# A dynamic convolution with a gated projection on one core: taps over pairs of groups, products grouped by tiling

## The chip, the core and the metric

The kernel runs on one core of a Trainium2 chip. The time is what one execution takes on the device, in microseconds (us). Three executions of the kernel before took 504.61, 506.79 and 507.75 us; their median, 506.79 us, is the time before.

## What is computed

The input x has 8 lanes (the batch) of 4224 positions of 192 channels, in fp32. Cut to what matters, the reference is:

```python
w = softmax(weight_gen, axis=-1)                   # 8 lanes x 4224 x 8 heads x 7 taps
x_unf[b, s, k] = x_pad[b, s + k]                   # 7 taps back in time, 24 channels per head
y = einsum('bshk,bskhg->bshg', w, x_unf)           # the dynamic convolution
for k in range(5): gate_pre += conv_w[k] * y_pad[:, k:k + S, :]
gate = 1 / (1 + exp(-gate_pre))
out = (gate * (y @ w_val)) @ w_out                 # w_val, w_out: 192 x 192
```

## The kernel before, in words

The sequence is cut into 36 groups of positions, g0 to g35: the first has 88, the last 56, all others 120. A group goes through these steps, for all 8 lanes at once.

**The softmax side.** weight_gen comes in 18 parts (p0 to p17). For each, VectorE takes the maximum, subtracts it, sums the exponentials, takes the reciprocal and normalises (lines 247 to 270), and ScalarE takes the exponential (257). SyncE's queue copies six rows between neighbours (the halo of a part, 241 and 242), ScalarE spreads the weights into lines with zeros between them (287), SyncE stores these lines to DRAM (304) and loads them back in slanted order into one of two tiles tb (351): so each group gets band matrices.

**The banks (365).** TensorE multiplies x of the group with its band matrices, in four banks of 32 matmul instructions each, in tiles of 32 columns. kind 0 and 1 hold heads 0 to 3 of lanes 0 to 3 and 4 to 7, kind 2 heads 4 and 5, kind 3 heads 6 and 7. They are made in the order 3, 2, 0, 1. ScalarE copies each bank out of PSUM (384): 0 and 1 into ringA, 2 into ringB, 3 into a tile S. Twelve small DMAs on POOL's queue then move pieces of S into rows of ringA and ringB that the 24-channel heads leave free (393, 395). Each bank takes one of three PSUM tiles of the pool ps_a in turn, so that the fourth bank of a group takes the tile of the first.

**The gate.** Tap 0 of the 5 taps is a ScalarE copy with a scale (413), taps 1 to 4 are VectorE multiply-adds (420) on an accumulator, aA (960 columns) for ringA and aB (480) for ringB. Then ScalarE takes the Sigmoid (425). The rings hold three groups in a row; where a group stands at the front, a copy of four columns makes the halo (400).

**The values and the outputs.** The value product (441 to 448) multiplies ringA and ringB with w_val: wva uses the whole array, wvd too, wvm tiles of 64 columns, wvb tiles of 64 rows. VectorE multiplies gate and value (459, 461). The output product (omm) is made in two halves k; each has a B part (485, tiles of 64 rows) and an A part (478, whole array). ScalarE copies it out (499, 496 for half of the last group) and SyncE stores it (511, 509).

**The order.** Nothing is scheduled by a tool: every step is put into a list with a planned time, and the list is sorted. Planned group m starts at when(m), 12.9 us after the one before; stage(m, t, ...) puts a step at when(m) + t. The engines follow the resulting order each in its own queue and wait for each other. Softmax steps of VectorE take the places (2.3, 10.4, 13.6) of each planned period, exponentials 7.05, spreads 5.0 or 11.6. The value product of a group stands one period after its banks, its outputs two periods after:

```python
stage(m + 1, 9.2, g.sigm, 1)
stage(m + 1, 10.4, g.sigm, 0)
stage(m + 1, 6.05 if m < NM - 1 else 3.6, g.val)
for k, t in ((0, 3.7), (1, 10.7))[:g.halves]:
    stage(m + 2, t, g.omm, k)
```

Of the kernel before, what the change touches and what calls it, by code (L numbers as in the profile page):

```python
# [17 lines left out]
def tile_dynconv_gated_moe(  # L18
# [15 lines left out]
    nc = tc.nc  # L34
# [36 lines left out]
    LP = HALO + 3 * NB  # L71
# [5 lines left out]
    ps_a = ctx.enter_context(tc.tile_pool(name="ps_a", bufs=3, space=bass.MemoryType.PSUM))  # L77
    ps_v = ctx.enter_context(tc.tile_pool(name="ps_v", bufs=1, space=bass.MemoryType.PSUM))
    ps_o = ctx.enter_context(tc.tile_pool(name="ps_o", bufs=1, space=bass.MemoryType.PSUM))
# [5 lines left out]
    ringA = const.tile([P, L, LP], FP32, name="ringA")  # L85
    ringB = const.tile([P, LH, LP], FP32, name="ringB")
# [9 lines left out]
    un01 = work.tile([P, 2, 2 * D], FP32, name="ot", bufs=4).bitcast(U32)  # L96
    un = [un01[:, :, 0:D], un01[:, :, D:2 * D], const.tile([P, 2, KC], U32, name="un")]
    raw_t = const.tile([P, 4 * NWT], FP32, name="raw")
# [208 lines left out]
    class Group:  # L307

        def __init__(self, m):
# [5 lines left out]
            self.p0 = HALO + NB * (m % 3) + (NB - self.n if m == 0 else 0)  # L315
            self.pa = {}
# [36 lines left out]
        def bank(self, kind):  # L353
# [6 lines left out]
            pa = ps_a.tile([P, 512], FP32, name="pa")  # L360
# [25 lines left out]
        def move(self, k, u):
            eng = nc.sync if self.m >= NM - 2 and u else nc.gpsimd
            g, q, ch = HOLE[k]
# [3 lines left out]
            if g == 0:  # L392
                eng.dma_start(out=ringA[q:q + h, LH * u:LH * u + LH, p0:p0 + n], in_=self.S[p:p + h])  # L393
            else:
                eng.dma_start(out=ringB[HD * u + q:HD * u + q + h, :, p0:p0 + n], in_=self.S[p:p + h])  # L395

        def halo(self, g):
            if self.m and self.m % 3 == 0:
                r = (ringA, ringB)[g]
                nc.scalar.copy(out=r[:, :, 0:HALO], in_=r[:, :, LP - HALO:LP])  # L400

        def src(self, g, j):
            p = self.p0 - HALO + j
            return (ringA, ringB)[g][:, :, p:p + self.n]

        def tap0(self, g):
            self.halo(g)
            n = self.n
            if g == 0:
                self.aA = work.tile([P, L * NB], FP32, name="aA", bufs=3)[:, 0:L * n]  # L410
            else:
                self.aB = work.tile([P, LH * NB], FP32, name="aB", bufs=3)[:, 0:LH * n]
            nc.scalar.activation(out=self.lanes(self.acc(g)), in_=self.src(g, 0), func=AF.Copy, scale=cw[:, g, 0:1])  # L413

        def acc(self, g):
            return self.aA if g == 0 else self.aB

        def tap(self, g, j):
            a = self.lanes(self.acc(g))
            nc.vector.scalar_tensor_tensor(out=a, in0=self.src(g, j), scalar=cw[:, g, j:j + 1], in1=a,  # L420
                                           op0=ALU.mult, op1=ALU.add)

        def sigm(self, g):
            a = self.acc(g)
            nc.scalar.activation(out=a, in_=a, func=AF.Sigmoid)  # L425

        def val(self):
            n = self.n
            if self.m == NM - 1:
                v2, *v01 = [ps_a.tile([P, 512], FP32, name="pa") for _ in range(3)]  # L430
            else:
                v2 = ps_v.tile([P, 512], FP32, name="v2")
                v = ps_v.tile([P, 2, 512], FP32, name="v01")
                v01 = [v[:, u] for u in range(2)]
                self.both = v
            self.v2, self.v01 = v2, v01
            A, Bt = self.src(0, HALO), self.src(1, HALO)
            A = [A[:, LH * u:LH * u + LH] for u in range(2)]
# [276 lines left out]
```

## Time and profile before

| | |
|---|---|
| median of three executions | 506.79 us |
| the profiled execution | 508.85 us |
| its span in the profile | 507.1 us |
| TensorE, VectorE, ScalarE, POOL busy | 467.9, 415.7, 337.1, 282.6 us |
| mean granted clock of TensorE | 0.972 of full speed |
| moved by DMA | 108.76 MB |

The profile is of one execution. PE is TensorE's matmuls, PEld its weight loads, DVE VectorE, ACT ScalarE, SPq the issues of SyncE's queue; L365 is line 365. A row of a timeline has the start in us from the span's start, the duration in us, the engine, the line, the operation, the tiles it writes and reads, the shape, the number of instructions merged into it, and in brackets the idle time before it with what released it. Matmuls are pipelined, so the distance between two starts says more than a duration. The rows named in the prediction stand in a section of their own below.

### The profile page before, as it was taken

Reading aid. Unit: us, or ns where it says so; the run is one execution under the profiler, and the core shown is the slowest. Engines: PE = TensorE matmul, PEld = TensorE weight load, DVE = VectorE, ACT = ScalarE, POOL = GpSimd, SP = SyncE. Lnnn points to the kernel's source line nnn. Section 1 sums busy time; section 2 is a strip of 40 time slices with the busy share of each in tenths; the row PEclk is TensorE's granted clock in tenths of the full one; section 3 lists DMA queues with packets and bytes.
Section 4 is the critical chain, followed back from the end, with each engine's and each line's share of the span. In section 5 each row is a group of like instructions: output and inputs, shape, how many; then the busy total and the mean of one; then the engine's idle time right before and its main releaser. Section 6 shows DMA issues by size and latency. Waiting matters only on the chain.

```text
span 507.1 us, 16002 instructions
## 1 busy us (share of the span) xinstructions
PE 467.9 (92%) x6338; PEld 330.2 (65%) x6338; DVE 415.7 (82%) x494; ACT 337.1 (66%) x524; POOL 282.6 (56%) x488
## 2 busy tenths in 40 slices
PE   9427699999999999999999999989999999999994
PEld 5325567666676767767677767757677776677663
DVE  7867789889896898898989899879879786677871
ACT  7346488968689468594959495759595565655632
POOL 9457545556564656556465656546566655556210
PEclk9867899999999999999999999999999999999989
DMA  6999999899899979798899999987978888886322
GB/s 202 224 198 276 235 211 239 228 217 224 205 221 257 230 190 212 233 267 210 232 251 252 235 250 226 233 218 199 223 219 225 208 206 222 232 223 183 94 76 90
DMA packets 117222, 108.76 MB, mean 214 GB/s; under 512 B 51920, under 2 KB 108363, under 8 KB 117149
## 3 DMA queue, kind: packets, MB, share of 16 engines
q1 hardware_dynamic: 96685, 74.37, 58.2%
q0 software_dynamic: 20464, 33.38, 26.7%
q8 instruction: 50, 0.82, 0.7%
q14 instruction: 23, 0.19, 0.1%
HBM read 60.39 MB, written 38.94 MB: 196 GB/s over the span
## 4 chain that ended last, share of the span: by engine, by line
DMA 39%; issue 14%; ACT 12%; POOL 12%; PE 11%; DVE 9%; SPq 2%; ACTq 0%; DVEq 0%; POOLq 0%
DMA ringB<-S 11%; DMA xt<-in_x_dram 10%; POOL ringA L393 9%; DMA ringA<-S 9%; DVE aA L420 5%; PE po L478 3%; DMA tb<-z 3%; PE pa L365 3%; DMA out_dram<-ot 3%; ACT zt L287 3%; DVE aB L420 2%; DMA wt<-in_weight_gen_dram 2%; PE po L485 2%; ACT L257 2%; DMA wt<-wt 1%
## 5 line engine op out<-in xcount | busy, mean ns | idle before, releaser
L393 POOL DMA_DIRECT2D ringA<-S x280 | 151.2, 546 | 99.5 <-DMA ringB<-S 30.2
L420 DVE SCALAR_TENSOR_TENSOR aA<-ringA,wf,aA 128x960 f32<-128x960 f32 (+2 forms) x144 | 171.3, 1190 | 38.4 <-ACT aA L413 31.9
L365 PE MATMUL pa<-tb,xt 126*32 126x120 f32 (+2 forms) x4608 | 137.5, 274 | 30.5 <-DMA tb<-z 19.4
L365 PEld LDWEIGHTS pa<-tb,xt 126*32 126x32 f32 (+2 forms) x4608 | 124.1, 111 | 43.0 <-issue 28.4
L395 POOL DMA_DIRECT2D ringB<-S x140 | 77.4, 557 | 91.7 <-ACT ringB L384 50.5
L420 DVE SCALAR_TENSOR_TENSOR aB<-ringB,wf,aB 128x480 f32<-128x480 f32 (+2 forms) x144 | 100.4, 697 | 16.5 <-ACT aB L413 14.3
L478 PE MATMUL po<-wf,aA 128*120 128x192 f32 (+2 forms) x560 | 112.0, 344 | 0.0
L478 PEld LDWEIGHTS po<-wf,aA 128*120 128x120 f32 (+2 forms) x560 | 90.6, 191 | 16.4 <-issue 13.6
L499 ACT COPY ot<-po 120x768 f32<-120x768 f32 (+1 forms) x69 | 55.4, 803 | 22.9 <-PE po L478 22.6
L425 ACT ACTIVATE aB<-aB 128x480 f32<-128x480 f32 (+2 forms) x36 | 21.5, 598 | 66.0 <-DVE aB L420 65.9
L441 PE MATMUL v<-ringA,wva 128*128 128x480 f32 (+1 forms) x140 | 62.4, 568 | 1.0 <-DMA ringB<-S 0.8
L485 PE MATMUL po<-wf,aB 64*120 64x192 f32 (+2 forms) x560 | 61.4, 338 | 0.0
L413 ACT ACTIVATE aA<-ringA,wf 128x960 f32<-128x960 f32 (+2 forms) x36 | 38.9, 1081 | 33.2 <-DMA ringA<-S 27.0
L485 PEld LDWEIGHTS po<-wf,aB 64*120 64x120 f32 (+2 forms) x560 | 46.8, 185 | 21.2 <-issue 18.2
L459 DVE TENSOR_TENSOR aA<-v,aA 128x960 f32<-128x960 f32 (+1 forms) x35 | 40.1, 1145 | 6.5 <-ACT aA L425 6.1
L425 ACT ACTIVATE aA<-aA 128x960 f32<-128x960 f32 (+2 forms) x36 | 35.8, 994 | 11.1 <-DVE aA L420 11.0
L287 ACT COPY zt<-wt 128x256 f32<-128x256 f32 (+3 forms) x80 | 37.5, 550 | 8.5 <-DVE wt L270 6.4
L448 PE MATMUL v<-ringB,wvb 64*128 64x480 f32 (+1 forms) x140 | 37.4, 611 | 0.0
L384 ACT COPY ringA<-pa 128x480 f32<-128x480 f32 (+2 forms) x72 | 35.9, 546 | 2.0 <-PE pa L365 2.0
L441 PEld LDWEIGHTS v<-ringA,wva 128*128 128x128 f32 x140 | 26.0, 193 | 16.4 <-issue 15.5
L327 POOL DMA_DIRECT2D xt<-in_x_dram x34 | 31.0, 911 | 9.5 <-DVE aA L459 3.8
L444 PE MATMUL v<-ringA,wvm 128*64 128x480 f32 (+1 forms) x140 | 35.7, 588 | 0.0
(84 smaller groups left out, 391.4 us busy)
## 6 DMA issues: line engine op xcount, KB each, us to landing
xt<-in_x_dram POOLq DMA_DIRECT2D x32, 768.0 KB, 7.9
out_dram<-ot SPq DMA_DIRECT2D x136, 180.0 KB
tb<-z SPq DMA_DIRECT2D x228, 88.0 KB
z<-zt SPq DMA_DIRECT2D x14, 576.0 KB
wt<-in_weight_gen_dram SPq DMA_DIRECT2D x14, 448.0 KB
ringA<-S POOLq DMA_DIRECT2D x268, 15.0 KB, 4.7
z<-zt SPq DMA_DIRECT2D x3, 800.0 KB
wt<-wt SPq DMA_DIRECT2D x14, 157.5 KB
```

Source lines behind the costliest of these rows:

```text
L287: nc.scalar.copy(out=dst, in_=src)
L365: nc.tensor.matmul(out=pa[Q * c:Q * c + Q, n * l:n * l + n], lhsT=self.xb[0:k, x0:x0 + Q], rhs=self.t[0:k, LH * u + l, PAD // 2:(PAD + n) ...
L393: eng.dma_start(out=ringA[q:q + h, LH * u:LH * u + LH, p0:p0 + n], in_=self.S[p:p + h])
L395: eng.dma_start(out=ringB[HD * u + q:HD * u + q + h, :, p0:p0 + n], in_=self.S[p:p + h])
L413: nc.scalar.activation(out=self.lanes(self.acc(g)), in_=self.src(g, 0), func=AF.Copy, scale=cw[:, g, 0:1])
L420: nc.vector.scalar_tensor_tensor(out=a, in0=self.src(g, j), scalar=cw[:, g, j:j + 1], in1=a, op0=ALU.mult, op1=ALU.add)
L425: nc.scalar.activation(out=a, in_=a, func=AF.Sigmoid)
L441: nc.tensor.matmul(out=v01[u][:, 0:w], lhsT=wva, rhs=A[u], start=True, stop=False)
L459: nc.vector.tensor_tensor(out=a, in0=self.both[:, :, 0:w], in1=a, op=ALU.mult)
L478: nc.tensor.matmul(out=po[0:n, u, D * t:D * t + D], lhsT=gA[:, u, k, t], rhs=woa, start=first and t == 0, stop=not first, skip_group_check ...
L485: nc.tensor.matmul(out=po[0:n, u, D * t:D * t + D], lhsT=gB[hs, k, t], rhs=wob[hs], start=first and t == 0, stop=not first, skip_group_che ...
L499: nc.scalar.copy(out=self.ot[0:n], in_=self.po[0:n, :, 0:2 * D])
```

## The change

- Taps: ringA and ringB get four slots, one for each group modulo 4, each with its own halo. An even group and the next odd one stand side by side; tap 0, the taps and the Sigmoid of the two are one instruction each, with twice the columns (1920 and 960). The first and the last two groups stay single. Halo copies are made for every pair.
- Values are made three periods behind the banks (two for the first two groups), outputs one period after them. At the end of the list the values of the last four groups and the outputs of the last five follow in turn.
- PSUM: one pool with tiles c (banks 3 and 0), v2 (bank 1 and the B values), v01 (the A values), x0 and x1 (the two halves of the output; x1 also bank 2).
- The products are split by tiling: both B parts of the output and wvb, then both A parts, wva, and last wvd with wvm.
- Softmax places move to (4.9, 10.4, 13.6), with places of their own in the first three periods; exponentials of later parts stand in even periods only. The tile ot has three buffers (before: four). The moves of the last group and the last stores are spread over three queues.

The core of the diff:

```diff
-    LP = HALO + 3 * NB
+    LP = HALO + NB
...
-    ringA = const.tile([P, L, LP], FP32, name="ringA")
-    ringB = const.tile([P, LH, LP], FP32, name="ringB")
+    ringA = const.tile([P, 4, L, LP], FP32, name="ringA")
+    ringB = const.tile([P, 4, LH, LP], FP32, name="ringB")
...
+            self.fast = m // 2 in (0, NM // 2 - 1)
...
-            pa = ps_a.tile([P, 512], FP32, name="pa")
+            pa = pair("x1")[:, 0] if kind == 2 else psum.tile([P, 512], FP32, name="v2" if kind == 1 else "c")
...
+            if self.m == NM - 1 and k < 4:
+                eng = (nc.gpsimd, nc.sync, nc.scalar)[(k + u) % 3]
...
-            if self.m and self.m % 3 == 0:
-                r = (ringA, ringB)[g]
-                nc.scalar.copy(out=r[:, :, 0:HALO], in_=r[:, :, LP - HALO:LP])
+            r, e = (ringA, ringB)[g], self.m % 4
+            if self.m % 2 == 0:
+                for a, b, n in ((1, 2, 2),) if e else ((3, 0, 1),) * (self.m > 0) + ((0, 1, 1),):
+                    nc.scalar.copy(out=r[:, b:b + n, :, 0:HALO].rearrange("p e l c -> p (e l) c"),
+                                   in_=r[:, a:a + n, :, NB:LP].rearrange("p e l c -> p (e l) c"))
...
+        def span(self, g, j):
+            if self.fast:
+                return self.src(g, j), self.lanes(self.acc(g))
+            i, e = (ringA, ringB)[g], self.m % 4
+            return (i[:, e:e + 2].rearrange("p e l c -> p (e l) c")[:, :, j:j + NB],
+                    self.sums[g].rearrange("p e (l n) -> p (e l) n", n=NB))
...
+        def val_w(self):
+            self.both = v = pair("v01")
             for u in range(2):
                 hs = slice(HD * u, HD * u + HD)
+                nc.tensor.matmul(out=v[:, u, 0:LH * self.n], lhsT=wvb[hs], rhs=self.src(1, HALO)[hs],
+                                 start=True, stop=False, tile_position=(HD * u, 0))
...
-            b_part(True)
-            a_part(False)
...
-                        nc.sync.dma_start(out=dst, in_=self.ot[h * e:h * e + h, u])
+                        (nc.gpsimd if e == 2 else (nc.scalar, nc.sync)[u]).dma_start(out=dst, in_=self.ot[k][h * e:h * e + h, u])
...
-    JOB, DENSE, EXP, SPREAD = (2.3, 10.4, 13.6), 0, (7.05,), (5.0, 11.6)
+    JOB, EXP, SPREAD = (4.9, 10.4, 13.6), (7.05,), (5.0, 11.6)
...
+    FIRST = ((10.4, 13.6), (4.9, 7.6, 10.4, 13.6), (2.3, 4.9, 6.0, 8.0, 10.4, 13.6))
...
-            at(slot(t, EXP), s.exp)
+            at(slot(t, EXP, 1 if i < 8 else 2), s.exp)
...
+        q = m // 2 * 2 + 2
+        if m < 2:
+            q = m + 1
+            stage(q, 1.5, g.tap0, 1)
+            stage(q, 2.15, g.tap0, 0)
...
+        elif m % 2 == 0:
+            end = m == NM - 4
+            stage(q, 1.5, g.tap0, 1)
+            stage(q, 2.65 if end else 4.85, g.tap0, 0)
+            for j in range(1, KC):
+                stage(q, (1.6, 3.0, 12.5, 13.6)[j - 1] if end else (1.6, 3.2, 3.3, 14.0)[j - 1], g.tap, 1, j)
+                stage(q, (2.7, 3.1, 12.4, 13.5)[j - 1] if end else (6.5, 12.5, 15.6, 17.4)[j - 1], g.tap, 0, j)
+            for k, t in ((1, 5.0), (0, 9.7)):
+                stage(q + 1, 5.6 - 0.1 * k if end else t, g.sigm, k)
+        late = m + 3 - (NM - 1)
+        if late >= 0:
+            t = 3.0 + 9.0 * late
+            stage(NM - 1, t, g.val_w)
+            stage(NM - 1, t + 0.1, g.val_a)
+            stage(NM - 1, t + 0.2, g.val_m)
...
+        else:
+            v = m + (3 if m > 1 else 2)
+            stage(v, 5.2, g.val_w)
+            stage(v, 8.6, g.val_a)
+            stage(v, 10.2, g.val_m)
+            stage(v, 11.7, g.gv, 0)
+            stage(v, 12.4, g.gv, 1)
...
+                stage(v + 1, 3.7 + 0.75 * k, g.omm_b, k)
+                stage(v + 1, 6.0 + 0.4 * k, g.omm_a, k)
+                stage(v + 1, 7.3 + 1.35 * k, g.oev, k)
+                stage(v + 1, 7.31 + 1.35 * k, g.store, k)
```

## Rows read from the trace of the kernel before

**Rows 1.** The head of the profile's page and its first part: busy us of each engine, its share of the span, and its instructions.

```profile
span 507.1 us, 16002 instructions
PE 467.9 (92%) x6338; PEld 330.2 (65%) x6338; DVE 415.7 (82%) x494; ACT 337.1 (66%) x524; POOL 282.6 (56%) x488
```

**Rows 2.** Stretches of the span: from and to, length, busy us and instructions of PE, PEld, DVE, ACT and POOL, then the granted clock of TensorE, the mean busy share of the 16 DMA engines and GB/s. The cuts are the starts of bank g0, g3 and g35 and one period in the middle.

```profile
23.39:68.92 45.53, 28.96 (x445) 21.61 (x445) 34.39 (x50) 24.49 (x48) 26.32 (x42) 0.76 1.01 230
68.92:273.46 204.54, 201.08 (x2786) 141.55 (x2785) 181.16 (x208) 153.87 (x228) 118.19 (x208) 1.00 0.92 230
273.46:477.81 204.35, 201.14 (x2785) 141.80 (x2784) 166.09 (x193) 134.57 (x215) 116.52 (x204) 1.00 0.84 215
477.81:507.10 29.29, 21.72 (x237) 16.00 (x236) 15.47 (x23) 10.20 (x18) 3.23 (x6) 0.92 0.26 79
```

**Rows 3.** The timeline of TensorE through one period in which it waited for nothing.

```profile
252.16 0.92 PE L485 MATMUL po<-wf,aB 64*120 64x192 f32 x8
253.01 1.57 PE L478 MATMUL po<-wf,aA 128*120 128x192 f32 x8
254.42 1.77 PE L441 MATMUL v<-ringA,wva 128*128 128x480 f32 x4
256.03 0.97 PE L442 MATMUL v<-ringB,wvd 128*128 128x480 f32 x2
256.92 1.03 PE L444 MATMUL v<-ringA,wvm 128*64 128x480 f32 x4
257.88 1.07 PE L448 MATMUL v<-ringB,wvb 64*128 64x480 f32 x4
258.79 0.82 PE L485 MATMUL po<-wf,aB 64*120 64x192 f32 x8
259.54 1.57 PE L478 MATMUL po<-wf,aA 128*120 128x192 f32 x8
261.03 3.62 PE L365 MATMUL pa<-tb,xt 126*32 126x120 f32 x128
264.58 0.92 PE L485 MATMUL po<-wf,aB 64*120 64x192 f32 x8
```

**Rows 4.** The same timeline, the start of bank g7 (bank g35 starts at 477.81, the cut in rows 2).

```profile
120.11 3.65 PE L365 MATMUL pa<-tb,xt 126*32 126x120 f32 x128
```

**Rows 5.** The view of waits: engine, its line, what it waited for, us in total, how often, the longest.

```profile
PEld pa L365 <- ACT S L384: 10.7, 13, 1.6
```

**Rows 6.** Timelines of TensorE and ScalarE around a bank that waited (bank g10 starts at 158.84), and the copy of S of the bank at 261.03, which came in time.

```profile
161.26 0.55 ACT L384 COPY S<-pa 128x480 f32<-128x480 f32 x1
...
161.87 1.05 PE L365 MATMUL pa<-tb,xt 126*32 126x120 f32 x32 [0.23 <-ACT S L384]
162.85 0.92 PE L485 MATMUL po<-wf,aB 64*120 64x192 f32 x8
...
262.20 0.57 ACT L384 COPY S<-pa 128x480 f32<-128x480 f32 x1 [0.19 <-PE pa L365]
```

**Rows 7.** The timeline of VectorE: three taps in a row.

```profile
280.41 1.21 DVE L420 SCALAR_TENSOR_TENSOR aA<-ringA,wf,aA 128x960 f32<-128x960 f32 x1
281.54 0.71 DVE L420 SCALAR_TENSOR_TENSOR aB<-ringB,wf,aB 128x480 f32<-128x480 f32 x1
282.17 1.21 DVE L420 SCALAR_TENSOR_TENSOR aA<-ringA,wf,aA 128x960 f32<-128x960 f32 x1
```

**Rows 8.** Groups of ScalarE's instructions by line and shape: count, busy us in all, mean ns of one, idle us before them and what ended it.

```profile
L499 ACT COPY ot<-po 120x768 f32<-120x768 f32 x67 | 53.8, 802 | 20.2 <-PE po L478 20.0
L413 ACT ACTIVATE aA<-ringA,wf 128x960 f32<-128x960 f32 x34 | 37.4, 1100 | 32.6 <-DMA ringA<-S 26.4 <-issue 4.8 <-ACT ringA L400 0.7
L413 ACT ACTIVATE aB<-ringB,wf 128x480 f32<-128x480 f32 x34 | 23.8, 701 | 0.4
L257 ACT ACT_TABLE_LOAD x14 | 18.0, 1283 | 0.2
L257 ACT ACTIVATE wt<-wt 128x896 f32<-128x896 f32 x14 | 13.3, 951 | 1.1 <-DVE wt L253 1.0
L400 ACT COPY ringA<-ringA 128x32 f32<-128x32 f32 x11 | 2.4, 219 | 0.0
```

**Rows 9.** The start: timelines of TensorE, VectorE and ScalarE, and one row of the chain that ended last (the halo copy of part 4).

```profile
53.49 0.88 DVE L459 TENSOR_TENSOR aA<-v,aA 128x704 f32<-128x704 f32 x1
...
57.95 0.62 PE L365 MATMUL pa<-tb,xt 126*32 126x120 f32 x16 [3.62 <-issue]
...
59.64 1.22 DVE L420 SCALAR_TENSOR_TENSOR aA<-ringA,wf,aA 128x960 f32<-128x960 f32 x1 [2.64 <-DMA ringB<-S]
...
79.42 1.08 DVE L270 TENSOR_TENSOR wt<-wt,mx 128x896 f32<-128x896 f32 x1
...
80.53 6.99 DMA wt<-wt
...
87.58 2.11 ACT L287 COPY zt<-wt 128x256 f32<-128x256 f32 x4 [1.06 <-DMA wt<-wt]
```

**Rows 10.** The end: a stretch behind bank g35 (columns as in rows 2), and SyncE's queue issuing the last stores.

```profile
480.90:486.40 5.50, 5.50 (x28) 4.22 (x21) 5.12 (x6) 1.99 (x4) 3.17 (x6) 0.69 0.32 85
...
501.18 3.49 SPq L509 DMA_DIRECT2D out_dram<-ot  x8
```

More of the change, by code (lines that the diff above doesn't have):

```diff
@@ L425, in sigm @@
             nc.scalar.activation(out=a, in_=a, func=AF.Sigmoid)
[L427 to L438, printed above, removed]
-            w = LH * n
-            for u in range(2):
-                nc.tensor.matmul(out=v01[u][:, 0:w], lhsT=wva, rhs=A[u], start=True, stop=False)
-            nc.tensor.matmul(out=v2[:, 0:w], lhsT=wvd, rhs=Bt, start=True, stop=True)
-            for u in range(2):
-                nc.tensor.matmul(out=v2[HD * u:HD * u + HD, 0:w], lhsT=wvm, rhs=A[u], start=False, stop=True,
-                                 tile_position=(0, HD * u), skip_group_check=True)
+        def val_w(self):
+            self.both = v = pair("v01")
@@ L446, in val, with val_a @@
             for u in range(2):
                 hs = slice(HD * u, HD * u + HD)
-                nc.tensor.matmul(out=v01[u][:, 0:w], lhsT=wvb[hs], rhs=Bt[hs], start=False, stop=True,
-                                 tile_position=(HD * u, 0))
+                nc.tensor.matmul(out=v[:, u, 0:LH * self.n], lhsT=wvb[hs], rhs=self.src(1, HALO)[hs],
+                                 start=True, stop=False, tile_position=(HD * u, 0))
+        def val_a(self):
+            A = self.src(0, HALO)
+            for u in range(2):
+                nc.tensor.matmul(out=self.both[:, u, 0:LH * self.n], lhsT=wva, rhs=A[:, LH * u:LH * u + LH],
+                                 start=False, stop=True)
@@ new lines, in val_m @@
+        def val_m(self):
+            w = LH * self.n
+            self.v2 = v2 = psum.tile([P, 512], FP32, name="v2")
+            A = self.src(0, HALO)
+            nc.tensor.matmul(out=v2[:, 0:w], lhsT=wvd, rhs=self.src(1, HALO), start=True, stop=False,
+                             skip_group_check=True)
+            for u in range(2):
+                nc.tensor.matmul(out=v2[HD * u:HD * u + HD, 0:w], lhsT=wvm, rhs=A[:, LH * u:LH * u + LH], start=False,
+                                 stop=True, tile_position=(0, HD * u), skip_group_check=True)
@@ L498, in oev @@
             else:
-                nc.scalar.copy(out=self.ot[0:n], in_=self.po[0:n, :, 0:2 * D])
+                nc.scalar.copy(out=ot[0:n], in_=po)
         def store(self, k):
@@ L571, in tile_dynconv_gated_moe, with slot @@
     at(0.9, lambda: stir(90))
-    JOB, DENSE, EXP, SPREAD = (2.3, 10.4, 13.6), 0, (7.05,), (5.0, 11.6)
+    JOB, EXP, SPREAD = (4.9, 10.4, 13.6), (7.05,), (5.0, 11.6)
     LAND = 11.0
     taken = set()
-    def slot(t, offs):
-        p, o = min((p, o) for p in range(1, NM) for o in offs if (p, o) not in taken and when(p) + o > t)
+    def slot(t, offs, step=1):
+        p, o = min((p, o) for p in range(step, NM, step) for o in offs if (p, o) not in taken and when(p) + o > t)
         taken.add((p, o))
@@ L586, in spread @@
             at(t + 0.6, s.halo, nc.sync)
[L587 removed]
+            t += 0.6 + (4.5 if s.i < 5 else 7.0 if s.i < 7 else LAND)
         for c in range(len(s.zc)):
@@ L629, in tile_dynconv_gated_moe @@
     at(c.ready + 0.005, gr[2].load_x)
-    slots = sorted(when(m) + o for m in range(1, NM) for o in (JOB if m > DENSE else (*JOB, 6.5)) if (m, o) > (1, 5.0))
+    FIRST = ((10.4, 13.6), (4.9, 7.6, 10.4, 13.6), (2.3, 4.9, 6.0, 8.0, 10.4, 13.6))
+    slots = sorted(when(m) + o for m in range(1, NM) for o in (JOB if m > 3 else FIRST[m - 1]))
     seq = []
```

139 lines of the change are left out of this document (69 added, 70 removed).

## The prediction

> **What bounds the kernel now.** I read the busy shares first [rows 1]: TensorE 92%, VectorE 82%, ScalarE 66%. An average over stages says little, so next the stretches [rows 2]. From 68.92 us, where bank g3 starts, to 477.81, where the last bank starts, TensorE is busy 402.2 of 408.9 us at a granted clock of 1.00. Before that it works 29.0 of 45.5 us while the 16 DMA engines are at 1.01, and after it 21.7 of 29.3. So the middle is bound by TensorE, the start by data, the end by TensorE with some gaps.
>
> One period of the middle, start to start [rows 3]: output product k=0 0.85 (its B part, 64-row tiles) + 1.41 (its A part, whole array); value product 1.61 (wva) + 0.89 (wvd) + 0.96 (wvm, 64-column tiles) + 0.91 (wvb, 64-row tiles); output product k=1 0.75 + 1.49; four banks (32-column tiles) 3.55. That is 12.42 us; other undisturbed periods are up to 0.1 longer, so I take 12.45. The measured mean from bank g7 to bank g35 is (477.81 - 120.11)/28 = 12.775 [rows 2, 4]. The missing 0.33 per period is one wait: TensorE waits for ScalarE's copy of S, 13 times, 10.7 us in all [rows 5]. The fourth bank takes the PSUM tile that the first one filled, and the copy is late when a spread or an exponential stands before it in ScalarE's queue.
>
> **The sum** goes by three pieces: when bank g7 starts, 28 periods, and what follows the start of bank g35. Before: 120.1 + 357.7 + 29.3 = 507.1, the profiled span. That execution took 508.85, 0.4% above the median 506.79; I carry the difference in us over to the median.
>
> **The period.** Ordering by tiling. Before there are six changes of tiling in a period (columns of 32, rows of 64, whole, columns of 64, rows of 64, whole, columns of 32); after there are four (both B parts and wvb together, then both A parts, wva and wvd, then wvm). A change costs what the same block takes longer with it than without: the A part 1.49 against 1.41 when whole-array work follows, the B part 0.85 against 0.75 when 64-row work precedes [rows 3]: 0.08 and 0.10. Two fewer: -0.18 (bounds 0 and -0.35, twice the row).
>
> The new wait. With PSUM regrouped, the first bank (S) and the third share one tile, "c", so the third bank now waits for the copy of S; the fourth is free. Undisturbed, the copy starts 1.17 after the bank (262.20 against 261.03 [rows 3, 6]), and TensorE resumed 0.61 after such a start (161.87 against 161.26 [rows 6]): 1.78, while two banks take 1.77. The wait itself is nothing, but a held bank also cost 0.10 to refill (162.85 - 161.87 = 0.98, against 0.885, a quarter of 3.55). So +0.12 every period (bounds 0 and +0.3). Queued behind it are the other banks and all of that period's products.
>
> The old wait. ScalarE was late because its Sigmoids stood in the queue waiting for VectorE's last tap. With values three periods behind, Sigmoid, tap 0 and gates have half a period or more in hand, and a spread or exponential has ended by the next copy: I count in the longer (even) period four bank copies (0.55 each [rows 6], 2.2), the two wide tap 0 (3.0, below) with up to four halo copies (0.9), two output copies (1.6), an exponential with its table load (2.2) [rows 8] and a spread (2.1 [rows 9]): 12.0 as durations, of which some 0.1 of each overlaps the next, so about 11 of 12.4 us. So of 0.33 I keep 0.02 (bounds 0 and the first rival's).
>
> Shared taps. An A tap starts 1.13 after the last, a B tap 0.63 [rows 7]: (1.13 - 0.63)/480 is 1.04 ns per element, 0.13 fixed. A pair saves 8 x 0.13 = 1.0 us of VectorE, 0.5 per period. On ScalarE tap 0 took 1.10 for 960 elements and 0.70 for 480 [rows 8], so 0.83 ns each and 0.30 fixed: 1.9 and 1.1 for a pair, 0.6 saved, somewhat less on the Sigmoids, about 16 us in all against 30 more halo copies at 0.22 = 6.6 us. Neither engine is the bound in the middle, so both stand at 0; without that cover VectorE's 10.6 per period would still lie under 12.4. SyncE's stores now come in pairs behind the output copies, ahead of the next loads of tb; those are issued two periods before their bank, which covers it. POOL's 12 moves per group and its x loads are unchanged; the ring of four slots only loosens them.
>
> New period: 12.45 - 0.18 + 0.12 + 0.02 = 12.41; 28 of them 347.5 (before 357.7).
>
> **The start.** By bank g7 the old kernel had done values g0 to g5 and outputs g0 to g4; the new one only to g3 and g2. So 2 x 4.4 + 2 x 4.5 = 17.8 us [rows 3] move from before bank g7 to behind the last bank; they are lost unless bank g7 comes that much earlier. How early it can come, step by step: the first A tap of g1 starts at 59.64, after the ring's moves and a stop of 3.6 us for which TensorE's row names no releaser [rows 9]; nothing in the change hastens that. Behind it VectorE now has seven taps (4 x 1.13, 3 x 0.63), two softmax steps, then sum 4, the two gate products of g0 (0.88 [rows 9] and half of it for B, 1.3), reciprocal 4 and normalisation 4, at some 1.05 a softmax step: 13 us, so g0's gates end at 70.3 and part 4 is normalised at 72.6 (before 80.5). Outputs of g0 hold TensorE until 70.3; with values g1 behind them bank g4 starts near 79.5. Part 4's halo copy (6.99) lands at 79.6, its spread (2.1) ends at 81.8 [rows 9], and S of bank g4 stands behind it: third bank 82.4, bank g5 88.8, bank g6 96.7. Outputs of g2 then need g2's gates, which lie behind eight wide taps (13 us) and seven softmax steps: 102.4. Bank g7: 102.4 + 8.8 = 111.2. Bounds: 104 without the stop and the last wait, 120.1 (as before) if the DMA engines, at 1.01, give nothing more.
>
> **The end.** Behind the start of bank g35: that bank 2.0, values of g32 to g34 3 x 4.3 and g35 2.1, outputs of g31 to g34 4 x 4.6 and g35 2.3 = 37.8, dense: gates of one group are made under the outputs of the one before. Then the last output copies and stores, which took 6.5. Eight of those stores were issued one after the other in 3.49 [rows 10]; three queues make that about 1.5 to 2 us less: 42.8 (bounds 42 and 46). Before, the same stretch with 17.8 us less work took 29.3, not least since it ran 5.5 us at a clock of 0.69 [rows 10].
>
> 111.2 + 347.5 + 42.8 = **501.5**, 5.6 us less than the span. 506.8 - 5.6 = **501**.
>
> **Rivals.**
> *Slower: the copy of S decides every period.* Its grace falls by one bank, 0.885 us. If ScalarE stays as late as before, 12 of 32 periods wait 0.87 + 0.885 and the rest 0.12: 12.27 + 0.73 = 13.0 a period, +16.5 us: 518. For it: the wait was there 13 times with more grace. Against it: ScalarE no longer waits for VectorE at the period's end. It turns the result to slower from a mean loss of 0.4 us a period. Chance 0.13.
> *The lead at the start doesn't come.* Bank g7 at 120, the products added behind the end: 120.1 + 347.5 + 42.8 = 510.4, on the median 510. For it: DMA at 1.01 of its time and 230 GB/s before 68.92 [rows 2]; against it: some of that is work for outputs that now come later. Chance 0.18.
> *TensorE starts slow.* With less work in the first periods it idles more. The rows show the price: in 23.39 to 68.92, half idle, the granted clock is 0.76 [rows 2], that is partly 1.2 GHz. If the 8 us periods g3 to g5 ran for half of their work at 1.2 GHz, bank g7 would come 4 to 6 us later: 506. Chance 0.07. The Trainium skill says this too (TensorE: Matmul & The Clock Gate, HAM oscillation): a kernel that puts idle gaps between bursts falls back to half clock again and again. By that rule 506, by the rows' mean alone 501; the trace agrees that gaps precede the low clock, and no row shows how the new gaps will lie.
> *More than forecast.* Bank g7 at 105, period 12.3, end 42: 491. The stop at 54 to 58 us need not recur, and four changes of tiling may cost less than I keep. Chance 0.17.
>
> **Numbers.** Forecast 0.45 (its own range 495 to 507), the rest as above. A change within 1% (about 5.1 us, what a measurement of this kernel can tell) is no change: 501.7 to 511.9. Faster: 0.28 of the forecast's 0.45 and all of the last rival, 0.45. Slower: the first rival and 0.05 of the second, 0.18. Same: 0.37. The range 490 to 515 leaves out the better half of the last rival and the worse half of the first.
>
> **What would show it.** In the new profile: the bank starts 12.3 to 12.5 apart in the middle; waits of TensorE for S before the third bank, short and in nearly every period; B parts, wvb, A parts, wva, wvd, wvm in one run of about 8.7; bank g7 near 111; about 38 us of TensorE behind the start of bank g35, at a clock of 1.00; VectorE near 400 busy. I am wrong if the period is above 12.6 (S), if bank g7 is beyond 116, or if the last stretch has gaps.

## The result, and the profile after

The changed kernel takes 513.5 us in the median of four runs, the kernel before 505.7 beside it (the three executions of above and a fourth, 504.04): a ratio of 1.0116, 95% interval 1.0067 to 1.0164. Ratios and intervals, here and in the table below, leave out executions that were longer for reasons outside the kernel; medians hold them all. It is slower by 1.2%, where I had forecast 1% faster; the time still lies inside the range. The profiled execution took 513.05 us, its span is 511.3.

The page's head and first part (rows 1 of before):

```profile
span 511.3 us, 15659 instructions
PE 463.6 (91%) x6338; PEld 332.6 (65%) x6338; DVE 404.4 (79%) x365; ACT 332.8 (65%) x488; POOL 282.5 (55%) x489
```

Stretches, columns as in [rows 2]; the cuts are the starts of banks g0, g4, g7 and g35 and the end of the last product:

```profile
23.77:84.75 60.98, 36.65 (x573) 28.13 (x573) 42.90 (x59) 31.95 (x61) 33.48 (x55) 0.69 1.00 219
84.75:119.49 34.74, 30.10 (x479) 22.27 (x477) 30.68 (x25) 27.52 (x40) 20.92 (x38) 0.95 0.99 215
...
119.49:461.93 342.44, 340.69 (x4874) 247.22 (x4873) 286.07 (x230) 243.31 (x346) 205.94 (x361) 1.00 0.92 230
461.93:503.00 41.07, 39.74 (x330) 25.20 (x328) 25.84 (x31) 15.57 (x24) 2.70 (x5) 1.00 0.29 87
503.00:511.30 8.30, 0.00 (x0) 0.00 (x0) 0.56 (x1) 0.48 (x1) 1.07 (x2) 0.63 0.23 69
```

The three pieces of my sum can be read off: 119.5 to the start of bank g7, 342.4 for 28 periods, 49.4 behind the start of bank g35. Before they were 120.1, 357.7 and 29.3; I had forecast 111.2, 347.5 and 42.8. So the middle gained 15.3 us, more than forecast, the start gained nothing, and the end lost 20.1.

One undisturbed period of the middle, TensorE's timeline (compare [rows 3]):

```profile
131.63 1.12 PE L368 MATMUL c<-tb,xt 126*32 126x120 f32 x32
132.57 1.05 PE L368 MATMUL x<-tb,xt 126*32 126x120 f32 x32
133.44 1.06 PE L368 MATMUL c<-tb,xt 126*32 126x120 f32 x32
134.31 1.05 PE L368 MATMUL v<-tb,xt 126*32 126x120 f32 x32
135.29 1.57 PE L486 MATMUL x<-wf,aB 64*120 64x192 f32 x16
136.70 0.97 PE L447 MATMUL v<-ringB,wvb 64*128 64x480 f32 x4
137.60 2.87 PE L495 MATMUL x<-wf,aA 128*120 128x192 f32 x16
140.30 1.77 PE L453 MATMUL v<-ringA,wva 128*128 128x480 f32 x4
141.91 0.97 PE L462 MATMUL v<-ringB,wvd 128*128 128x480 f32 x2
142.81 1.03 PE L465 MATMUL v<-ringA,wvm 128*64 128x480 f32 x4
143.77 1.10 PE L368 MATMUL c<-tb,xt 126*32 126x120 f32 x32
```

It is 12.14 us; most others are 12.05 to 12.14, where before the undisturbed ones were 12.42 to 12.54. Both B parts now take 1.41 (0.85 + 0.75 before), both A parts 2.70 (1.41 + 1.49). The third bank starts 1.81 behind the first, and the copy of S is there.

The view of waits, TensorE:

```profile
PE c L368 <- DMA tb<-z: 25.2, 3, 11.0
PE v L368 <- DVE aB L474: 4.5, 4, 3.2
PE c L368 <- DMA xt<-in_x_dram: 3.2, 1, 3.2
PE c L368 <- ACT S L387: 2.4, 3, 1.5
```

The same view of the kernel before has:

```profile
PE pa L365 <- ACT S L384: 7.5, 11, 1.3
```

So the matmuls' wait for S fell from 7.5 us in 11 waits to 2.4 in 3. (The 10.7 in 13 of [rows 5] is PEld's row, the weight loads; they have 3.6 in 5 now.) New waits stand in the start: the fourth bank of g3 waits 3.2 us for the B gate of g0 (both use the PSUM tile v2), and bank g6 waits 3.2 for its x.

### The profile page after: what moved, and what is told of

It is laid out like the page before. It is cut to its first block, busy times and chain, and to the rows that moved or that the text cites. A ratio compares the mean times of both kernels' runs of the same rounds, so it can differ in the third digit from the quotient of the medians.

```text
span 511.3 us, 15659 instructions
## 1 busy us (share of the span) xinstructions
PE 463.6 (91%) x6338; PEld 332.6 (65%) x6338; DVE 404.4 (79%) x365; ACT 332.8 (65%) x488; POOL 282.5 (55%) x489
## 4 chain that ended last, share of the span: by engine, by line
PE 36%; DMA 34%; issue 14%; POOL 8%; ACT 3%; DVE 3%; SPq 1%; POOLq 0%; ACTq 0%
DMA ringB<-S 9%; PE x L495 8%; DMA xt<-in_x_dram 7%; PE c L368 6%; DMA tb<-z 5%; POOL ringA L398 5%; DMA out_dram<-ot 5%; PE x L486 5%; PE v L453 5%; DMA ringA<-S 5%; PE v L368 3%; PE x L368 3%; PE v L447 3%; PE v L465 2%; PE v L462 2%
## 5 line engine op out<-in xcount | busy, mean ns | idle before, releaser
L437 DVE SCALAR_TENSOR_TENSOR aA<-ringA,wf,aA 128x1920 f32<-128x1920 f32 (+3 forms) x80 | 157.8, 1973 | 10.6 <-ACT aA L430 9.0
L368 PE MATMUL c<-tb,xt 126*32 126x120 f32 (+2 forms) x2304 | 81.4, 282 | 30.8 <-DMA tb<-z 25.2
L495 PEld LDWEIGHTS x<-wf,aA 128*120 128x120 f32 (+2 forms) x568 | 91.1, 188 | 24.1 <-issue 24.0
L495 PE MATMUL x<-wf,aA 128*120 128x192 f32 (+2 forms) x568 | 103.0, 334 | 0.0
L437 DVE SCALAR_TENSOR_TENSOR aB<-ringB,wf,aB 128x960 f32<-128x960 f32 (+3 forms) x80 | 88.4, 1105 | 17.7 <-ACT aB L430 15.4
L368 PEld LDWEIGHTS c<-tb,xt 126*32 126x32 f32 (+2 forms) x2304 | 62.5, 114 | 59.1 <-issue 26.1
L506 ACT COPY ot<-x 120x768 f32<-120x768 f32 (+1 forms) x70 | 54.4, 796 | 55.7 <-PE x L495 29.4
L453 PE MATMUL v<-ringA,wva 128*128 128x480 f32 (+2 forms) x144 | 64.3, 570 | 0.0
L486 PE MATMUL x<-wf,aB 64*120 64x192 f32 (+2 forms) x568 | 58.3, 343 | 0.0
L486 PEld LDWEIGHTS x<-wf,aB 64*120 64x120 f32 (+2 forms) x568 | 45.9, 188 | 10.0 <-issue 8.9
```

The costliest lines, as they stand in the source:

```text
L368: nc.tensor.matmul(out=pa[Q * c:Q * c + Q, n * l:n * l + n], lhsT=self.xb[0:k, x0:x0 + Q], rhs=self.t[0:k, LH * u + l, PAD // 2:(PAD + n) ...
L437: nc.vector.scalar_tensor_tensor(out=o, in0=i, scalar=cw[:, g, j:j + 1], in1=o, op0=ALU.mult, op1=ALU.add)
L453: nc.tensor.matmul(out=self.both[:, u, 0:LH * self.n], lhsT=wva, rhs=A[:, LH * u:LH * u + LH], start=False, stop=True)
L486: nc.tensor.matmul(out=po[0:n, u, D * t:D * t + D], lhsT=gB[hs, k, t], rhs=wob[hs], start=t == 0, stop=False, skip_group_check=True, tile_ ...
L495: nc.tensor.matmul(out=self.po[k][0:n, u, D * t:D * t + D], lhsT=gA[:, u, k, t], rhs=woa, start=False, stop=True, skip_group_check=True)
L506: nc.scalar.copy(out=ot[0:n], in_=po)
```

## The experiments

My theory after reading this profile: the order by tiling gains in the middle; the added depth moves products from a start that data hold to behind the last bank, where they cost all they take. Rivals: the pairs, TensorE's low clock in the start, GpSimd's queue (x loads, last stores), and the shared PSUM tile of S. The pieces of the profiled executions (all but e12's), and the times against the kernel before on the same chip:

| kernel | g7 starts | 28 periods | behind g35 | span | median | ratio, interval |
|---|---|---|---|---|---|---|
| before | 120.1 | 357.7 | 29.3 | 507.1 | 505.7 to 507.8 | |
| changed | 119.5 | 342.4 | 49.4 | 511.3 | 513.5 | 1.012, 1.007 to 1.016 |
| e1_stores_sp | 118.9 | 344.6 | 46.4 | 509.9 | 511.4 | 1.012, 1.004 to 1.021 |
| e2_no_order | 120.1 | 361.3 | 47.7 | 529.1 | 531.0 | 1.051, 1.042 to 1.060 |
| e3_singles | 115.4 | 343.7 | 47.7 | 506.7 | 512.5 | 1.014, 1.004 to 1.023 |
| e4_old_depth | 123.9 | 354.3 | 31.4 | 509.6 | 514.5 | 1.016, 1.004 to 1.028 |
| e5_old_depth_own_s | 126.9 | 367.3 | 31.0 | 525.2 | 525.3 | 1.034, 1.025 to 1.042 |
| e6_own_s | 116.7 | 349.9 | 47.7 | 514.3 | 515.2 | 1.015, 1.008 to 1.021 |
| e7_x_early | 119.9 | 344.6 | 48.2 | 512.7 | 514.6 | 1.016, 1.009 to 1.024 |
| e8_stir | 118.4 | 341.6 | 47.7 | 507.7 | 513.5 | 1.011, 1.007 to 1.015 |
| e9_one_deeper | 123.0 | 350.3 | 36.7 | 510.0 | 512.0 | 1.010, 1.004 to 1.016 |
| e10_no_early_products | 110.1 | 346.5 | 47.7 | 504.3 | 506.1, one execution | |
| e11_late_gate | 123.7 | 355.1 | 29.0 | 507.7 | 508.2 | 1.002, 0.998 to 1.005 |
| e12_gate_first | – | – | – | – | 505.0 | 0.997, 0.994 to 1.000 |
| e13_two_queues | 116.7 | 345.5 | 46.5 | 508.6 | 509.4 | 1.003, 0.999 to 1.007 |
| e14_gate_two_queues | 124.6 | 351.4 | 27.9 | 503.9 | 504.3 | 0.992, 0.988 to 0.996 |

Changed, e1 and e13 do the same up to bank g7 and have it at 116.7 to 119.5: a difference of 3 us between two single profiles of the start says little.

**The order undone.**

```
-                stage(v + 1, 6.0 + 0.4 * k, g.omm_a, k)
+                stage(v + 1, 3.75 + 0.75 * k, g.omm_a, k)
```

> Changed kernel with each A part of an output product right behind its B part again, so eight changes of tiling in a period for four. Theory (a change costs what the middle gained, 12.45 - 12.14 = 0.31 us for two, 0.155 each): four more cost 0.62 us a period, the undisturbed period is 12.75, bank g7 to bank g35 takes 342 + 17 = 359 us, the time 530. Rival (a change costs 0.09 as I forecast, and the rest of the middle's gain is a shorter bank wait): 12.50, 352 us, 523. Other rival (order is worth nothing, the gain is all from the depth that took the wait for S away): 342 us, 513.

One period of its timeline of TensorE:

```profile
253.02 0.92 PE L486 MATMUL x<-wf,aB 64*120 64x192 f32 x8
253.87 1.57 PE L495 MATMUL x<-wf,aA 128*120 128x192 f32 x8
255.36 0.92 PE L486 MATMUL x<-wf,aB 64*120 64x192 f32 x8
256.22 1.57 PE L495 MATMUL x<-wf,aA 128*120 128x192 f32 x8
257.71 1.08 PE L447 MATMUL v<-ringB,wvb 64*128 64x480 f32 x4
258.72 1.88 PE L453 MATMUL v<-ringA,wva 128*128 128x480 f32 x4
...
265.90 0.92 PE L486 MATMUL x<-wf,aB 64*120 64x192 f32 x8
```

From 253.02 to 265.90 are 12.88 us, 0.76 more than the 12.12 with the order: 0.19 for each of four changes. The blocks show where: the B and A parts 4.69 for 4.11, wvb 1.01 for 0.90, wva 1.71 for 1.61 (its next row starts at 260.43). The theory had 359 us for the 28 periods and a time of 530; measured were 361.3 and 531. The Trainium skill says that changing the tiling mode drains TensorE (TensorEngine Tiling (Array Packing), Key Properties) and gives no price; these rows agree, and they price it. So the order is what makes the middle faster; with eight changes, two more than before, the kernel takes 5% longer than before.

**The pairs undone**, two single operations at the place of each pair's:

```
-            self.fast = m // 2 in (0, NM // 2 - 1)
+            self.fast = True
...
-            stage(q, 1.5, g.tap0, 1)
+            for h in (g, gr[m + 1]):
+                stage(q, 1.5, h.tap0, 1)
...
```

> Changed kernel with every tap operation and Sigmoid for one group again, two behind each other at the place of the pair's, depth and order kept. Theory (pairs only relieve VectorE and ScalarE, which do not bound the middle): VectorE's busy time rises by some 16 us and the time stays within 513 +- 2 us. Rival (the pairs give the room in ScalarE's queue that keeps the copy of S in time): waits of TensorE for S come back, up to 0.3 us a period, 520 or more. Other rival (a wide tap holds the gates up, TensorE waits for them in the start): bank g7 comes 1 to 2 us earlier, 511.

VectorE rose from 404.4 to 416.2 us, the middle is 343.7 for 342.4, the time 512.5 for 513.5. The pairs relieve an engine that does not bound. Bank g7 at 115.4 lies 1.3 us below the scatter given above, so the other rival, 1 to 2 us by a wide tap in the start, is not excluded.

**The depth undone**, order and PSUM kept (pairs undone too; softmax slots, the moves of the last group and the last stores as before):

```
-            v = m + (3 if m > 1 else 2)
...
+        stage(m + 1, 9.2, g.sigm, 1)
+        stage(m + 1, 10.4, g.sigm, 0)
+        t = (5.2, 8.6, 10.2) if m < NM - 1 else (3.6, 3.6, 3.6)
+        stage(m + 1, t[0], g.val_w)
...
+            stage(m + 2, 3.7 + 0.75 * k, g.omm_b, k)
+            stage(m + 2, 6.0 + 0.4 * k, g.omm_a, k)
```

> Products ordered by tiling and the new PSUM, but no pairs, values one period and outputs two behind the convolution as before, softmax slots and last stores as before. Theory (the depth loses: 17.8 us of products moved from the start, where they lay under the data's time, to behind the last bank): bank g7 at 120 as before, the stretch behind the start of bank g35 back to 29 to 30 us, the period between 12.2 and 12.4, so 120 + 344 + 29.5 = 494 us and up to 498. Rival (the depth is what keeps the copy of S in time; without it the wait is back and with one bank less of grace): period 12.7 to 13.0, 505 to 513 us. Other rival (the start and the end lose by the new PSUM tiles and the clock, not by the depth): bank g7 at 119 but the last stretch above 40 us, 505 or more.

Here a rival was right. The end came back to 31.4, but the middle took 354.3 with undisturbed periods of 12.1 and waits for S between them. ScalarE's and TensorE's timelines at one of them:

```profile
133.94 0.60 ACT L439 ACTIVATE aB<-aB 128x480 f32<-128x480 f32 x1 [0.42 <-DVE aB L435]
135.07 1.00 ACT L439 ACTIVATE aA<-aA 128x960 f32<-128x960 f32 x1 [0.53 <-DVE aA L435]
136.50 2.21 ACT L288 COPY zt<-wt 128x256 f32<-128x256 f32 x4 [0.43 <-DMA wt<-wt]
138.61 0.56 ACT L387 COPY S<-c 128x480 f32<-128x480 f32 x1
...
139.23 1.04 PE L368 MATMUL c<-tb,xt 126*32 126x120 f32 x32 [1.26 <-ACT S L387]
```

The Sigmoids wait for VectorE's last taps, the spread for a halo, and the copy of S stands behind them all. That is my first rival, in its place and as often as it said (12 waits), but cheaper: 0.2 to 2.2 us a time, 12.7 in all, where it had 1.76 a time. The depth, with the softmax slots that go with it, is what keeps it from happening; the pairs are not (e3 has 343.7 us in the middle without them). Against e1, which has the same last stores, the depth (with pairs and slots) is worth 9.7 us in the middle and 5.0 in the start, and costs 15.0 at the end: in sum nothing.

**A PSUM tile for S alone**, with the old depth (e5) and with the new one (e6):

```
-            pa = pair("x1")[:, 0] if kind == 2 else psum.tile([P, 512], FP32, name="v2" if kind == 1 else "c")
+            pa = (pair("x0" if kind == 2 else "x1")[:, 0] if kind in (0, 2) else
+                  psum.tile([P, 512], FP32, name="v2" if kind == 1 else "c"))
```

> e4_old_depth with one thing more: S has its PSUM tile to itself (the third bank takes a half of x1 and the second one of x0), so a copy of S may be late by a whole period. Theory (at the old depth all that is left of the loss is the wait for S: 12.7 us in 12 waits, 1.1 to 1.5 each in the middle, and 2.2 + 1.7 in the start): no wait for S, middle 28 x 12.15 to 12.25 = 340 to 343 us for 354.3, bank g7 at 120 for 123.9, the rest 31 as there: 491 to 495 us of span, some 497 in the median, 2% under the kernel before. Rival (ScalarE's queue is simply too full at the old depth; then the same lateness shows at the next tile, x0 or x1 waiting for the output copies or the bank copies): middle stays at 350 or more, 508 or more.

> Changed kernel, pairs and depth kept, S with its PSUM tile to itself as in e5. Theory (with the depth ScalarE is hardly late, so this is worth the few waits for S and x: 1.5 in the start and some 1.5 to 4 in the middle): middle 340 to 341 us, bank g7 at 117 to 118, the last stretch unchanged at 49, so 507 to 508 of span, 510 in the median. Rival (the waits for S in the start are what kept the lead from coming): bank g7 at 112 to 114, 505.

In e5 no bank waits for S, and the view of waits has this in its place:

```profile
PE x L485 <- ACT ringA L388: 17.7, 17, 3.6
```

The lateness of ScalarE moved one tile on, to the third bank's copy that the B part of k=1 waits for, and grew: the rival held. In e6 the waits for S are gone too, and others (v2, x) leave the middle at 349.9 and bank g7 at 116.7, so neither theory nor rival held. Another tile is no cure for a queue that is late.

**Two suspects of the start.** Dummy matmuls in TensorE's idle time (e8), x loads ahead of the moves (e7):

```
+        if m in (1, 2):
+            stage(m, -0.01, stir, (0, 40, 30)[m])
```

```
-            stage(m - 1, -4.0, g.load_x, nc.gpsimd)
+            stage(m - 2, 2.0, g.load_x, nc.gpsimd)
```

> Changed kernel with 40 and 30 matmuls of zeros that nothing reads in the idle time of TensorE before banks g1 and g2. Rival of mine (TensorE starts slow: half clock in the start is what keeps the lead from coming): granted clock from 39 to 66 us rises from 0.62 to 0.69 to 0.9 or more, banks there take 0.9 instead of 1.6 us each, and bank g7 comes 3 to 5 us earlier, at 115. Theory (the start waits for data, moves and VectorE, not for TensorE): the clock rises, the banks get shorter, and bank g7 stays within 118 to 120; 512 to 514 us.

> Changed kernel with GpSimd issuing each load of x before the moves of the group two ahead of it instead of behind them. Theory (bank g6 waited 3.2 us for an x load that stood behind the moves of g4): that wait goes, the low clock that came behind it too (1.5 us), bank g7 at 115 instead of 119.5, the middle unchanged or up to 2 us longer as the moves are issued 1 to 2 us later; 509 to 511 us. Rival (the DMA engines are full in the start, whichever transfer goes first another is late): bank g7 stays at 118 to 120 with the wait on tb or on the moves, 513.

The stretch from bank g1 to bank g3, in e8:

```profile
37.68:64.90 27.22, 19.70 (x301) 14.44 (x301) 16.46 (x20) 11.88 (x21) 16.45 (x26) 0.84 1.04 227
```

and in the changed kernel:

```profile
39.13:66.41 27.28, 17.21 (x270) 13.62 (x270) 18.56 (x22) 13.80 (x23) 16.81 (x27) 0.65 1.09 235
```

The granted clock rose from 0.65 to 0.84, the stretch stayed 27.2 us long with the DMA engines at 1.04, and bank g7 came at 118.4. The clock was a result of the idling, not what held this stretch. Of the periods behind it e8 says little. There the changed kernel ran at the lower of TensorE's two levels, 1.2 GHz, behind each of its two waits of 3.2 us:

```profile
72.51:78.61 6.10, 6.10 (x53) 4.02 (x53) 4.28 (x5) 4.16 (x5) 3.96 (x8) 0.51 0.72 155
105.93:109.14 3.21, 3.21 (x65) 3.07 (x69) 2.61 (x3) 1.85 (x5) 2.61 (x5) 0.50 0.93 191
```

The blocks in the first stretch took 2.8 us longer than the same blocks at full clock, those in the second 1.4. In e8 the clock was low behind the first wait too (0.66 from 73 to 78 us).

In e7 the wait for x is gone, and this stands in its place, on ScalarE and TensorE:

```profile
103.27 1.28 ACT L258 ACT_TABLE_LOAD   x1
104.56 0.97 ACT L258 ACTIVATE wt<-wt 128x896 f32<-128x896 f32 x1
105.55 1.28 ACT L441 ACT_TABLE_LOAD   x1
106.84 1.80 ACT L441 ACTIVATE aA<-aA 128x1920 f32<-128x1920 f32 x1
108.55 0.54 ACT L387 COPY S<-c 128x480 f32<-128x480 f32 x1
...
109.15 1.04 PE L368 MATMUL c<-tb,xt 126*32 126x120 f32 x32 [2.32 <-ACT S L387]
```

An exponential between the two wide Sigmoids costs two more table loads, and the copy of S is late instead of x: the third bank of g6 starts at 109.15, in the changed kernel, where the same loads stand beside the wait for x, at 109.14. Bank g7 stays at 119.9, though the clock is 1.00 here from 104.80 us to its start: the 1.4 us of low clock are gone with the wait for x and bring nothing. The 2.8 us no run takes away.

**The start without products.**

```
+        if m < 4:
+            continue
         late = m + 3 - (NM - 1)
```

> Changed kernel without the values, gates, outputs and stores of groups g0 to g3 (they are left out altogether, 31 us of TensorE's work, most of which stood before bank g7). If TensorE's work sets the start, as my sum had it, bank g7 comes 20 us or more earlier, at 90 to 99. Theory (data, moves, softmax and ScalarE's queue set it): bank g7 at 108 to 116, that is at most 10 us for 31 us of work. The middle at 342, the last stretch unchanged.

Bank g7 starts at 110.1: with 31 us of products gone, of which all but the outputs of g3 (4.1 us) stood before bank g7, it comes 9.4 us earlier, 0.30 to 0.35 for each us. That is rather too low, since TensorE's clock fell with the idling: 0.75 from 84 us to bank g7, where the changed kernel has 0.95. Even with none of them it would come only 1.1 us before the time I had forecast with them. TensorE's waits up to bank g7 (the view of waits, that stretch alone):

```profile
PE c L368 <- DMA tb<-z: 26.5, 3, 9.7
PE c L368 <- ACT S L387: 10.3, 3, 5.3
PE c L368 <- DMA z<-zt: 6.9, 1, 6.9
PE c L368 <- DMA wt<-wt: 5.5, 1, 5.5
PE c L368 <- ACT wt L258: 3.9, 1, 3.9
```

Loads, the halo copy, the exponential and ScalarE's queue: without products, the softmax chain holds the start. e4 against e1 gives nearly the same rate, 17.8 us of products, 5.0 us of bank g7, 0.28; but these two differ in more than the depth, and 3 of the 5 us may be scatter.

**Half of the depth** (values two, outputs three behind, Sigmoids in the second period; on e4):

```
+        v = m + (2 if 1 < m < NM - 1 else 1)
+        fast = m < 2 or m >= NM - 2
+        stage(m + 1 if fast else v, 9.2 if fast else 4.9, g.sigm, 1)
...
```

> e4_old_depth with values two periods and outputs three behind the convolution (from group 2 on; the last group as there), Sigmoids in the second period, tap operations for single groups: half of the depth that the change adds. Theory (depth gains in the middle because a Sigmoid no longer stands in ScalarE's queue waiting for VectorE's last tap, and loses at the end what it moves there; one period of depth is enough for the first and moves only 8.9 us): middle 340 to 345 us, bank g7 at 117 to 120, the stretch behind the start of bank g35 at 36 to 38 us, span 496 to 500, median 498 to 502, 1 to 2% under the kernel before. Rival (the wait for S goes only with two periods): middle at 350 or more, 508 or more. Other rival (products done early delay the start as much as they save at the end): bank g7 at 124 or more, 505.

The end is where the theory had it (36.7), the middle, at 350.3, in between, the start at 123.0: 510.0. The waits for S are nearly gone from the middle, as the theory had it (1.0 us in two waits); the fourth bank's wait for the B gate (3.9) and waits for output copies (2.1) stand there instead. With e4 (509.6) and e1 (509.9) that makes three depths of the same span: as far as single profiles tell, each period of depth trades the end against the middle and the start at par.

**The queue's order in place of depth.** e11 (on e4) puts the A Sigmoid and the spread behind the copy of S; e12 moves that Sigmoid directly behind it:

```
-        stage(m + 1, 10.4, g.sigm, 0)
+        stage(*((m + 1, 10.4) if end else (m + 2, 1.6)), g.sigm, 0)
...
-        stage(m + 1, 11.7, g.gv, 0)
+        stage(*((m + 1, 12.4) if end else (m + 2, 2.4)), g.gv, 0)
...
-    JOB, EXP, SPREAD = (2.3, 10.4, 13.6), (7.05,), (5.0, 11.6)
+    JOB, EXP, SPREAD = (2.3, 10.4, 13.6), (7.05,), (5.0, 2.7)
```

```
-        stage(*((m + 1, 10.4) if end else (m + 2, 1.6)), g.sigm, 0)
+        stage(*((m + 1, 10.4) if end else (m + 2, 0.97)), g.sigm, 0)
...
```

> e4_old_depth with ScalarE's queue set in another order, no depth added: the A Sigmoid and the spread stand behind the next copy of S instead of ahead of it, the A gate follows that Sigmoid, and the B taps come earlier in VectorE's period. Theory (what the depth gains in the middle is only that nothing which waits for VectorE or for a halo stands ahead of the copy of S): the 12 waits for S go without any depth, middle 340 to 346 us for 354.3, bank g7 at 118 to 121, the rest 30 to 31 as in e4, span 489 to 498, median 491 to 500, 1.5 to 3% under the kernel before. Rival (at the old depth the chain bank, moves, taps, Sigmoid, gate, output does not fit the period and the lateness only moves): waits for gates or at x in place of those for S, middle at 350 or more, 508 or more.

> e11_late_gate with the A Sigmoid directly behind the copy of S (ahead of tap 0 of B) and the A gate ahead of the first B tap. Theory (in e11 the wait for S is gone and 0.4 to 0.7 us in every other period is left, wvb waiting for the A gate that reads the same PSUM): those waits go, middle 346 to 350 us for 355, bank g7 and the last stretch unchanged, 500 to 504 in the median, about 1% under the kernel before. Rival (the middle without depth is now held by data, the DMA share being 0.92 to 0.95 there, or by VectorE): the waits move to another operand and the middle stays at 353 or more, 508.

The ratio to the kernel before fell from e4's 1.016 to 1.002 and 0.997, less than expected, and e11's profiled middle did not shrink (355.1, as its rival had it): the lateness partly moved, to wvb and the A gate in e11, to S again with e12's order (7.0 us in 10 waits in e14). What would bring the middle of 342 at this depth stays open.

**The last stores.** One queue (e1), two (e13, and e14 on e12), where the change has three:

```
-                        (nc.gpsimd if e == 2 else (nc.scalar, nc.sync)[u]).dma_start(out=dst, in_=self.ot[k][h * e:h * e + h, u])
+                        nc.sync.dma_start(out=dst, in_=self.ot[k][h * e:h * e + h, u])
```

```
+                        (nc.scalar, nc.sync)[u].dma_start(out=dst, in_=self.ot[k][h * e:h * e + h, u])
```

> Changed kernel with all eight last stores on SyncE's queue again. Theory (stores spread over three queues cost time, since those on GpSimd's queue are issued slowly and land late): the stretch behind the last product falls from 8.3 to about 6.5 us, the time from 513 to 511, nothing else moves. Rival (the last output copies, not the queue, set that stretch): it stays at 8.3 us or grows by the 1.5 to 2 us that the spreading was to save.

> Changed kernel with the last stores on ScalarE's and SyncE's queues alone, none on GpSimd's. Theory (the spreading works, and only GpSimd's queue makes the end late): the stretch behind the last product is 4.7 to 5.5 us for 8.3, the time 510. Rival (any second queue is slow to finish): 7 us or more. The bank g7 at 115 to 120, the middle at 342 to 345 and TensorE behind bank g35 at 39.4 to 41 as before.

> e12_gate_first with the last stores on two queues. Theory: the stretch behind the last product 4.7 to 5.5 us for 6.5, the rest as e12, so 1.3 us less: 503.5 to 504 in the median, 0.5 to 0.6% under the kernel before. Rival (any second queue is slow to finish): 505 to 506.

Behind the last product the change takes 8.3 us, e1 6.4, e13 5.4, e14 5.2. The DMA engines' busy tenths in 40 equal slices from 503 us to the end of the span, the changed kernel first, then e1, then e13:

```profile
DMA  8976100608488864000000000000000000000000
```

```profile
DMA  7988897520081036081441714516145000000000
```

```profile
DMA  9878876400017307686675473550000000000000
```

With three queues the last bytes move at 506.5 (17 slices of 0.21) and the span ends 4.8 us later; with one at 508.4 and 1.5 later; with two at 506.8 and 1.8 later. The spreading works; a store on GpSimd's queue at the very end costs 2.9 us (8.3 for 5.4).

Why it does, the trace shows, though not in the views, which leave such instructions out. At the end of the program GpSimd executes a drain. It takes 6.0 to 6.6 us in every kernel here and starts behind GpSimd's last issue. In e1 and e13 that is at 467.5 and 466.1 us, so it is long over at the end; in the changed kernel it starts at 504.38 and ends at 510.47, while SyncE is through with all its waits at 507.6. The seven kernels with three queues all have 8.3 us behind the last product except e7, with 8.8: there the drain took 6.60 for 6.09. So e1's theory named the right queue and the wrong reason: the stores on it landed 2.2 us after their issue.

e14, order without depth and two store queues, beats both kernels: 0.992 (0.988 to 0.996) of the time before.

## Why the prediction was wrong

*What bounds the kernel* held: TensorE is busy 340.7 of 342.4 us in the middle.

*The period* was wrong on the good side. The 0.33 that I gave to one wait I had read from the row of the weight loads; the matmuls waited for S only 5.5 us in the 28 periods, 0.20 each. The order was the term mis-sized: I took 0.09 for a change of tiling, from what one block loses beside another, and got -0.18; two changes gave 0.33, near my bound of 0.35 (e2: 0.19 each). The new wait, +0.12, is not there: 0.9 us in two waits over 28 periods. The waits left in the middle, 1.7 us of all kinds, and a few longer periods make 12.12 to 12.23.

*Shared taps* at 0 held (e3); VectorE came at 404, forecast near 400.

*The start* is the step that failed: bank g7 at 111.2, measured 119.5. I let it follow from TensorE's and VectorE's queues. Up to part 4's normalisation they went about as I had them: it ran at 73.67 to 74.76, forecast to end by 72.6. But the fourth bank of g3 waited 3.2 us for v2, which I had not followed through its new owner; that bank, both B parts of g0 and wvb of g1 behind it took 6.1 us for 3.3, at a granted clock of 0.51; x stood in GpSimd's queue; the table loads stood in ScalarE's. e7 shows that these lie behind one another, so that taking one away uncovers the next, and e10 that products decide little: the start gives back about 0.3 us for a us of products removed, not the half that I had. My second rival, that the lead doesn't come, is what happened. The clock, my third, had a part: I had 4 to 6 us for it in g3 to g5, and TensorE lost 2.8 and 1.4 us to it behind the two stops. e8 clears it up to bank g3 and e7 at g6; whether bank g7 would come earlier without the 2.8 us behind the stop at g3, or the next wait would take the gain, stays open.

*The end* is the second: 42.8, measured 49.4, beyond its bound of 46. TensorE's part was 41.0 for 37.8, with two waits (0.73 and 0.54), values of 4.6 for 4.3 and outputs of 4.7 for 4.6, since nothing is grouped by tiling there (wvb 1.01, wva 1.71, as in e2). The rest is the stores: 8.3 for the 5 that I had. I counted only the time to issue them, and not GpSimd's drain behind its last issue; with two queues they take 5.4 (e13).

*The first rival* had the right mechanism for the new PSUM without the depth (e4). So the books against the kernel before are: 15.3 us gained in the middle, of which the order is 0.33 x 28 = 9 and the rest the wait for S, which the new PSUM made worse (12.7 us in e4 for 7.5) and the depth avoids; 0.6 gained in the start; 20.1 lost at the end, of which 15.0 are the products that the depth moves there (e1 against e4) and 2.9 GpSimd's drain.

*The range.* Against my 501.5 of span the start missed by +8.3, the end by +6.6 and the period by -5.1 us. That the time lies inside the range is in part luck: an order worth more than I gave it paid for a third of the two misses. Two of the signs that I had named for being wrong came, bank g7 beyond 116 and gaps in the last stretch.

## What to carry to other kernels

Added depth moves work from the start to behind the last load. It is free only where the engine whose work is moved sets the start: leave the moved work out altogether and see how far the first full period moves; here 31 us of it moved 9.4. When a copy is late, ask first what stands ahead of it in its queue and waits for somebody else; another buffer or more depth treats the lateness, and pays elsewhere. Group TensorE's work by tiling. Leave the last stores to queues other than GpSimd's, so that its drain at the end of the program runs under other work.

## What the hardware showed beyond what I expected

A change between tilings of TensorE in fp32 cost 0.17 us (two fewer against before) to 0.19 (four more in e2). With a last store on GpSimd's queue the span stayed open for 4.8 us after the last byte, with SyncE's and ScalarE's alone for 1.5 to 1.8: GpSimd's drain, 6.0 to 6.6 us in all sixteen kernels, starts only behind its last issue. The Trainium skill says that all issuing engines share the same 16 DMA engines and that spreading saves only the time to issue (DMA: Bandwidth & Descriptors, Issuing engines are not separate DMA queues): for two queues the rows agree, 6.4 us became 5.4; with GpSimd's as a third the bytes were as early (3.5 us behind the last product, 3.6 with two), and the drain made the end later. Not settled: why bank g7 comes 4 to 7 us later in the kernels with the old depth and the new PSUM (123.7 to 126.9) than in the kernel before (120.1).
